# A planner's longer instruction fetch, the order of the first row loads, and the engine of the memory copy in a 68-step recurrent attention kernel

## The chip, the cores and the metric

The kernel runs on one core of a Trainium2 chip. A core has TensorE (PE in the profile; its weight loads are a row of their own, PEld), VectorE (DVE), ScalarE (ACT), GpSimd (POOL), SyncE (SP, which here only issues transfers) and 16 DMA engines. The metric is the device time of one execution in microseconds (us). Seven executions of the kernel before lie between 1632.25 and 1633.52 us, with a median of 1632.38 us.

## The reference

Four layers follow one another on a sequence of 2048 rows of 512 bf16 values: attention with a carried memory, a dense layer, the same attention again, the same dense layer again. Each reads the layer norm of its input and adds to it.

```python
for s in range(64):                                   # 64 segments of 32 rows
    h = concat([mem, xs])                             # 8 memory rows + 32 rows of the segment
    q, k, v = h @ Wq, h @ Wk, h @ Wv                  # 32 heads of 128
    p = softmax(where(mask, q @ k.T * scale, -1e9))
    o = (p @ v) @ Wo                                  # 40 x 512
    mem = o[:8]; outs.append(o[8:])                   # the memory goes into the next segment
x = x + attention(layernorm(x), mem0)
x = x + relu(layernorm(x) @ w1) @ w2                  # inner width 1376
# ... and both once more
```

The memory makes the segments of one attention layer a chain: a segment's queries, keys and values need the eight rows that the segment before it left.

## The kernel before

The two attention layers run side by side, the second four segments (DELTA) behind the first, so there are 68 steps. In steps 0 to 3 only the first is active, in steps 64 to 67 only the second, between them both. A step holds, for five units of heads (UNITS: u0 to u4): projections of queries and keys (`queries_keys`, PE line 667), values (`values`, PE line 1000), scores (line 1084), the softmax on DVE and ACT (`block`, `top`, `sub`, `exp`, `total`, `recip`, `mul`: lines 1095 to 1126), the turning of the probabilities on PE (`scores.turn`) with two masked copies out of PSUM (`keep`, lines 1149 on ACT and 1151 on DVE), the product with the values (`attend`, line 1168), and the output projection (`project`, PE into the bank `st`). In odd steps a pair of segments is finished and its dense layer begins; that work is spread over the next step too. The last matmuls of a dense layer (`dense_layer.mm.3` to `.5`) stream 512 columns each.

At a step's end `project` leaves the new memory in `st`, and one copy (`ev`, line 1212, on DVE: 128 x 64 values when both layers are active) brings its rows into HT, from which the next step's queries and keys are made. The rows of the segment itself are copied after it (`rows`, on ACT or DVE).

At the start, the weights come in through POOL's queue (Wv, then Wq, Wk and Wo in two pieces each; Wv's first quarter through SP). The rows of group 0 (128 rows) and the initial memory come through ACT's queue (`get_x`, `get_memory`, lines 619 and 622), as do the rows of groups 1 to 7 (`load`, line 827), into two buffers in turn. In steps 0 and 1 the values of those seven groups are made ahead of time (`*values`, PE line 1000), kept in the room of w1 and w2, and stored to DRAM by POOL (lines 838 and 963); then SP loads w1 and w2 into that room (`load_dense`).

Nothing of the order is written out by hand. `Plan.order` is a list scheduler: each operation has a cost on each engine that may do it, latencies between engines (LAT), and a priority from the tables PLACE, AHEAD and PERIOD. It walks through planned time, takes the operation of least priority that can start, and so fixes the order on every engine, the engine of each copy that either ACT or DVE may do (`copy_op`), and, for the operations in PAIRED, whether PE does a product in one go over 128 columns of weights or in two halves of 64 (twice the instructions; a change between the two shapes is a switch, planned at TURN). The planned times are used for nothing else. PE's instructions are modelled in `order` too: every 64 pairs of weight load and matmul are a block, and a block is not planned to end sooner than FETCH (7.0 us) after the fourth block before it.

Of the kernel before, what the change touches and what calls it, by code (L numbers as in the profile page):

```python
# [28 lines left out]
BLOCK, FETCH = 64, 7.0  # L29

RULE = (0.0714, 334.5336, 21842.5159, 2217302446.7678)
PERIOD = 40.244
PLACE = {
    ("attend.mmu0.0", 0): 609.348, ("attend.mmu0.0", 1): -183.486, ("attend.mmu0.0", 2): 147.437,
    ("attend.mmu0.0", 3): -78.515, ("attend.mmu0.0", 4): 65.61, ("attend.mmu0.0", 5): 366.858,
    ("attend.mmu0.0", 6): -249.718, ("attend.mmu1.0", 0): 726.903, ("attend.mmu1.0", 1): 684.118,
    ("attend.mmu1.0", 2): -19.8, ("attend.mmu1.0", 3): 132.658, ("attend.mmu1.0", 4): 129.759,
    ("attend.mmu1.0", 5): 371.411, ("attend.mmu1.0", 6): -353.4, ("attend.mmu2.0", 0): -14.873,
    ("attend.mmu2.0", 1): -1055.665, ("attend.mmu2.0", 2): 375.184, ("attend.mmu2.0", 3): 495.749,
    ("attend.mmu2.0", 4): 267.365, ("attend.mmu2.0", 5): 143.496, ("attend.mmu2.0", 6): -164.881,  # L40
    ("attend.mmu3.0", 0): 55.83, ("attend.mmu3.0", 1): 304.958, ("attend.mmu3.0", 2): -27.575,
    ("attend.mmu3.0", 3): 521.565, ("attend.mmu3.0", 4): -53.654, ("attend.mmu3.0", 5): -33.75,
    ("attend.mmu3.0", 6): 139.713, ("attend.mmu4.0", 0): -1004.936, ("attend.mmu4.0", 1): -1157.418,
    ("attend.mmu4.0", 2): -270.186, ("attend.mmu4.0", 3): -964.038, ("attend.mmu4.0", 4): -328.51,
    ("attend.mmu4.0", 5): 58.406, ("attend.mmu4.0", 6): -138.434, ("dense_layer.mm.0", 1): 844.726,
    ("dense_layer.mm.0", 3): 771.51, ("dense_layer.mm.0", 6): 794.222, ("dense_layer.mm.1", 1): 595.059,
    ("dense_layer.mm.1", 3): 282.976, ("dense_layer.mm.1", 6): -365.611, ("dense_layer.mm.2", 1): 402.759,
    ("dense_layer.mm.2", 3): 201.475, ("dense_layer.mm.2", 6): 383.89, ("dense_layer.mm.3", 1): 375.463,
    ("dense_layer.mm.3", 3): 375.816, ("dense_layer.mm.3", 6): 544.49, ("dense_layer.mm.4", 1): -1179.846,
    ("dense_layer.mm.4", 3): -271.405, ("dense_layer.mm.4", 6): -220.579, ("dense_layer.mm.5", 1): 907.374,  # L50
    ("dense_layer.mm.5", 3): 373.845, ("dense_layer.mm.5", 6): 565.451, ("finish_pair.turn.0", 1): -90.833,
    ("finish_pair.turn.0", 3): -375.688, ("finish_pair.turn.0", 6): -738.706, ("g0", 2): -581.803,
    ("g1", 2): -1043.701, ("g2", 2): 282.751, ("g3", 2): -205.545, ("g4", 2): 584.676, ("g5", 2): -60.649,
    ("g6", 2): 371.668, ("g7", 2): 288.938, ("late_values.mmv0.0", 0): -64.904, ("late_values.mmv1.0", 0): 678.294,
    ("late_values.mmv2.0", 0): 101.482, ("late_values.mmv3.0", 0): 44.512, ("late_values.mmv4.0", 0): 351.071,
    ("late_values.mmv5.0", 0): -24.294, ("late_values.mmv6.0", 0): -120.477, ("late_values.mmv7.0", 0): -996.402,
    ("layernorm.turn.0", 1): 92.873, ("layernorm.turn.0", 3): -23.204, ("layernorm.turn.0", 6): 193.698,
    ("layernorm.turn.1", 1): 910.291, ("layernorm.turn.1", 3): -857.558, ("layernorm.turnr.0", 0): -337.322,
    ("layernorm.turnr.1", 0): -831.277, ("prepare.turns.0", 2): 390.358, ("project.mm.0", 0): 359.615,
    ("project.mm.0", 1): -869.571, ("project.mm.0", 2): -60.568, ("project.mm.0", 3): -169.635,  # L60
    ("project.mm.0", 4): 156.569, ("project.mm.0", 5): 430.997, ("project.mm.0", 6): -293.953,
    ("project.mm.1", 0): 824.231, ("project.mm.1", 1): 252.725, ("project.mm.1", 2): 43.429,
    ("project.mm.1", 3): 540.792, ("project.mm.1", 4): -164.609, ("project.mm.1", 5): 588.5,
    ("project.mm.1", 6): 101.76, ("project.mm.2", 0): 126.782, ("project.mm.2", 1): -862.581,
    ("project.mm.2", 2): -235.851, ("project.mm.2", 3): 70.544, ("project.mm.2", 4): -259.138,
    ("project.mm.2", 5): -117.671, ("project.mm.2", 6): -300.67, ("project.mm.3", 0): 223.614,
    ("project.mm.3", 1): -213.188, ("project.mm.3", 2): -93.552, ("project.mm.3", 3): 545.141,
    ("project.mm.3", 4): 351.716, ("project.mm.3", 5): -238.608, ("project.mm.3", 6): -107.853,
    ("project.mm.4", 0): 230.883, ("project.mm.4", 1): -148.91, ("project.mm.4", 2): -568.124,
    ("project.mm.4", 3): 379.873, ("project.mm.4", 4): -132.884, ("project.mm.4", 5): 770.552,  # L70
    ("project.mm.4", 6): 66.643, ("queries_keys.mmu0.0", 0): -119.1, ("queries_keys.mmu0.0", 1): -850.808,
    ("queries_keys.mmu0.0", 2): -204.722, ("queries_keys.mmu0.0", 3): -113.926, ("queries_keys.mmu0.0", 4): 59.817,
    ("queries_keys.mmu0.0", 5): -235.287, ("queries_keys.mmu0.0", 6): -320.902,
    ("queries_keys.mmu0.1", 0): -402.058, ("queries_keys.mmu0.1", 1): 10.017, ("queries_keys.mmu0.1", 2): 261.017,
    ("queries_keys.mmu0.1", 3): -213.134, ("queries_keys.mmu0.1", 4): -297.361, ("queries_keys.mmu0.1", 5): -84.629,
    ("queries_keys.mmu0.1", 6): -888.993, ("queries_keys.mmu0.2", 0): -392.541,
    ("queries_keys.mmu0.2", 1): -333.397, ("queries_keys.mmu0.2", 2): -356.282, ("queries_keys.mmu0.2", 3): -51.387,
    ("queries_keys.mmu0.2", 4): -331.518, ("queries_keys.mmu0.2", 5): -853.492,
    ("queries_keys.mmu0.2", 6): -1044.343, ("queries_keys.mmu0.3", 0): -40.65, ("queries_keys.mmu0.3", 1): -57.543,
    ("queries_keys.mmu0.3", 2): -41.34, ("queries_keys.mmu0.3", 3): -1060.763, ("queries_keys.mmu0.3", 4): -376.858,  # L80
    ("queries_keys.mmu0.3", 5): -120.052, ("queries_keys.mmu0.3", 6): -111.195,
    ("queries_keys.mmu1.0", 0): -259.357, ("queries_keys.mmu1.0", 1): -373.272, ("queries_keys.mmu1.0", 2): 371.489,
    ("queries_keys.mmu1.0", 3): -1015.198, ("queries_keys.mmu1.0", 4): 169.449,
    ("queries_keys.mmu1.0", 5): -376.609, ("queries_keys.mmu1.0", 6): -35.359, ("queries_keys.mmu1.1", 0): -890.304,
    ("queries_keys.mmu1.1", 1): -52.862, ("queries_keys.mmu1.1", 2): 261.214, ("queries_keys.mmu1.1", 3): -931.873,
    ("queries_keys.mmu1.1", 4): -80.004, ("queries_keys.mmu1.1", 5): -905.415, ("queries_keys.mmu1.1", 6): -75.569,
    ("queries_keys.mmu1.2", 0): -1032.537, ("queries_keys.mmu1.2", 1): -941.562,
    ("queries_keys.mmu1.2", 2): -245.647, ("queries_keys.mmu1.2", 3): -738.459, ("queries_keys.mmu1.2", 4): 282.479,
    ("queries_keys.mmu1.2", 5): -47.448, ("queries_keys.mmu1.2", 6): -355.274, ("queries_keys.mmu1.3", 0): -1042.76,
    ("queries_keys.mmu1.3", 1): -311.787, ("queries_keys.mmu1.3", 2): -329.768,  # L90
    ("queries_keys.mmu1.3", 3): -856.085, ("queries_keys.mmu1.3", 4): -47.655, ("queries_keys.mmu1.3", 5): -394.586,
    ("queries_keys.mmu1.3", 6): -257.527, ("queries_keys.mmu2.0", 0): -51.901, ("queries_keys.mmu2.0", 1): -283.405,
    ("queries_keys.mmu2.0", 2): -257.559, ("queries_keys.mmu2.0", 3): 302.184, ("queries_keys.mmu2.0", 4): 98.406,
    ("queries_keys.mmu2.0", 5): 305.605, ("queries_keys.mmu2.0", 6): 363.104, ("queries_keys.mmu2.1", 0): -34.459,
    ("queries_keys.mmu2.1", 1): 44.98, ("queries_keys.mmu2.1", 2): 334.384, ("queries_keys.mmu2.1", 3): -1093.708,
    ("queries_keys.mmu2.1", 4): -293.392, ("queries_keys.mmu2.1", 5): 351.704,
    ("queries_keys.mmu2.1", 6): -1178.673, ("queries_keys.mmu2.2", 0): -41.303, ("queries_keys.mmu2.2", 1): 58.94,
    ("queries_keys.mmu2.2", 2): 291.775, ("queries_keys.mmu2.2", 3): 52.266, ("queries_keys.mmu2.2", 4): -151.786,
    ("queries_keys.mmu2.2", 5): 228.689, ("queries_keys.mmu2.2", 6): 405.936, ("queries_keys.mmu2.3", 0): 330.979,
    ("queries_keys.mmu2.3", 1): 57.914, ("queries_keys.mmu2.3", 2): -40.37, ("queries_keys.mmu2.3", 3): 87.416,  # L100
# [1234 lines left out]
```

## Time and profile before

| | us |
|---|---|
| profiled execution, whole | 1633.52 |
| its span, first to last instruction | 1631.8 |
| PE busy | 1588.3 (97%), 43116 matmuls |
| DVE busy | 1045.8 (64%) |
| ACT busy | 1077.9 (66%) |
| POOL busy | 139.6 (9%) |
| end of step 0, 1, 2, 3 | 56.27, 74.06, 95.55, 113.69 |
| a steady even step, a steady odd step | 24.82, 22.5 to 23.2 |
| median of seven executions | 1632.38 |

A step's end is the start of the first weight load after the last one of `project`. In the views below, "A <- B" means that A waited and B released it. A line is that of the helper that issued the instruction, so PE's line 667 covers projections, turnings and dense products alike, told apart by the tile that they write (work, st, fill). "Issue" is a wait for which the profile shows no releaser. PEclk is the granted clock of PE, 1.00 being full speed. Counting instructions gives one more measure: PE's weight loads are all in the trace, in the order of the program, so each planned operation can be found with its start.

### The profile page before, as it was taken

The numbers are of one execution on the slowest core, as the hardware profiler recorded it, in microseconds if no ns is written. First come the engines' busy times: TensorE is split into PE (matmuls) and PEld (weight loads), VectorE is DVE, ScalarE is ACT, GpSimd is POOL, SyncE is SP. The second block draws the span as 40 slices with busy tenths as digits, with TensorE's granted clock in tenths as the row PEclk, the third lists the DMA queues.
The fourth block names the chain that finished last, engine by engine and source line by source line (L and its number), as shares of the span: only waits on it lengthen the run. The fifth ranks groups of instructions, "written<-read, shape, count | busy, mean of one in ns | idle before, by whom it ended". The sixth has DMA issues, their size and how long they took to land.

```text
span 1631.8 us, 94544 instructions
## 1 busy us (share of the span) xinstructions
PE 1588.3 (97%) x43116; PEld 1381.0 (85%) x43179; DVE 1045.8 (64%) x3025; ACT 1077.9 (66%) x2717; POOL 139.6 (9%) x363
## 2 busy tenths in 40 slices
PE   7999999999999999999999999999999999999997
PEld 4778888888888888888888888888888888888886
DVE  4556656666765676676567567656656765665664
ACT  4556766766666676666667667666666666676654
POOL 4210000001000000100000000000000000000000
PEclk9999999999999999999999999999999999999998
DMA  9521001111100110111011111101101000000000
GB/s 372 198 82 35 19 23 28 25 25 35 31 23 21 30 25 25 35 28 26 22 30 25 25 35 28 25 23 28 26 25 26 25 19 19 20 18 19 16 6 6
DMA packets 42881, 63.30 MB, mean 39 GB/s; under 512 B 15401, under 2 KB 28817, under 8 KB 42481
## 3 DMA queue, kind: packets, MB, share of 16 engines
q1 hardware_dynamic: 35984, 35.88, 9.0%
q0 software_dynamic: 5328, 20.32, 3.3%
q8 instruction: 338, 5.54, 1.4%
q10 hardware_dynamic: 1168, 1.06, 0.2%
q14 instruction: 63, 0.51, 0.1%
HBM read 33.50 MB, written 11.93 MB: 28 GB/s over the span
## 4 chain that ended last, share of the span: by engine, by line
PE 92%; DVE 4%; DMA 1%; issue 1%; ACT 1%; POOL 0%; DVEq 0%; POOLq 0%; ACTq 0%; SPq 0%
PE work L667 38%; PE st L667 19%; PE fill L1000 15%; PE fill L667 12%; PE work L1168 4%; PE work L1084 3%; DMA hT<-in_A_x_dram 1%; DVE es L1095 1%; DVE sm L1109 1%; DVE mx L1099 1%; DVE P L1126 0%; DVE es L1102 0%; DVE HT L1212 0%; PE fill L791 0%; DMA xb<-in_A_x_dram 0%
## 5 line engine op out<-in xcount | busy, mean ns | idle before, releaser
L667 PE MATMUL work<-HT,Wk_sb 128*128 128x80 bf16 (+2 forms) x10144 | 363.7, 200 | 9.9 <-DVE HT L1212 9.2
L667 PE MATMUL work<-HT,Wq_sb 128*128 128x80 bf16 (+2 forms) x9728 | 361.7, 200 | 0.3 <-DVE HT L1212 0.2
L667 PEld LDWEIGHTS <-Wk_sb 128*128 128x128 bf16 (+1 forms) x10144 | 330.9, 103 | 29.9 <-DVE HT L1212 12.8
L667 PE MATMUL st<-OT,Wo_sb 128*128 128x80 bf16 (+1 forms) x8704 | 339.3, 199 | 1.9 <-ACT OT L921 1.3
L667 PEld LDWEIGHTS <-Wq_sb 128*128 128x128 bf16 (+1 forms) x9728 | 327.1, 102 | 13.4 <-DVE HT L1212 5.0
L667 PEld LDWEIGHTS <-Wo_sb 128*128 128x128 bf16 x8704 | 319.1, 99 | 11.0 <-issue 4.0
L1000 PE MATMUL fill<-Wv_sb,HT 128*64 128x512 bf16 x2176 | 274.0, 383 | 0.0
L921 ACT CAST kT<-work 128x320 bf16<-128x320 f32 (+1 forms) x537 | 219.4, 409 | 71.6 <-PE work L667 35.1
L921 ACT CAST qT<-work 128x320 bf16<-128x320 f32 (+1 forms) x484 | 197.3, 408 | 103.1 <-PE work L667 58.6
L1149 ACT ACTIVATE PT<-work,half 128x160 bf16<-128x160 f32 (+2 forms) x447 | 202.6, 468 | 18.2 <-DVE PT L1151 14.1
L921 ACT CAST OT<-work 128x320 bf16<-128x320 f32 (+1 forms) x387 | 149.2, 415 | 98.0 <-PE work L1168 97.9
L921 ACT CAST vw<-fill 128x512 bf16<-128x512 f32 x229 | 134.0, 585 | 104.5 <-PE fill L1000 102.3
L1095 DVE TENSOR_TENSOR es<-work,maskb 128x320 f32<-128x320 f32 (+2 forms) x340 | 130.5, 400 | 87.6 <-PE work L1084 80.7
L1000 PEld LDWEIGHTS <-HT 128*64 128x64 bf16 x2176 | 107.3, 110 | 72.5 <-issue 1.9
L1106 ACT ACTIVATE es<-es 128x320 f32<-128x320 f32 (+2 forms) x340 | 133.2, 406 | 8.3 <-DVE es L1102 3.5
L1126 DVE TENSOR_TENSOR P<-es,sm 128x320 bf16<-128x320 f32 (+2 forms) x337 | 131.1, 405 | 4.4
L1151 DVE TENSOR_SCALAR PT<-work,half 128x320 bf16<-128x320 f32 (+2 forms) x233 | 105.0, 454 | 44.5 <-PE work L667 42.6
L1102 DVE TENSOR_TENSOR es<-es,mx 128x320 f32<-128x320 f32 (+2 forms) x340 | 131.5, 403 | 1.5
L1099 DVE TENSOR_REDUCE mx<-es 128x8 f32<-128x320 f32 (+2 forms) x340 | 129.5, 397 | 2.8
L1109 DVE TENSOR_REDUCE sm<-es 128x8 f32<-128x320 f32 (+2 forms) x340 | 128.4, 393 | 1.8 <-ACT es L1106 1.7
L1212 DVE CAST HT<-st 128x64 bf16<-128x64 f32 (+1 forms) x67 | 14.8, 220 | 162.9 <-PE st L667 162.6
L1168 PE MATMUL work<-PT,vw 128*64 128x80 bf16 (+1 forms) x1384 | 106.0, 202 | 1.7 <-DVE PT L1151 1.7
(99 smaller groups left out, 1730.9 us busy)
## 6 DMA issues: line engine op xcount, KB each, us to landing
V<-vw SPq DMA_DIRECT2D x240, 48.0 KB
V<-vh SPq DMA_DIRECT2D x120, 64.0 KB
Wq_sb<-in_A_Wq_dram POOLq DMA_DIRECT2D x2, 2048.0 KB, 20.2
Wk_sb<-in_A_Wk_dram POOLq DMA_DIRECT2D x2, 2048.0 KB, 24.6
Wo_sb<-in_A_Wo_dram POOLq DMA_DIRECT2D x2, 2048.0 KB, 35.8
vh<-vg SPq DMA_DIRECT2D x32, 128.0 KB
Wv_sb<-in_A_Wv_dram POOLq DMA_DIRECT2D x1, 2048.0 KB, 11.5
vh<-w_sb POOLq DMA_DIRECT2D x4, 512.0 KB, 6.5
```

Source lines behind the costliest of these rows:

```text
L667: nc.tensor.matmul(out_[u:v, :], lhsT=lhsT[:, u:v], rhs=rhs, start=start, stop=stop, tile_position=(0, u), **more)
L921: nc.scalar.copy(out=out_, in_=in_)
L1000: nc.tensor.matmul(vp[64 * b:64 * b + 64, :], lhsT=cols(c4), rhs=Wv_sb[:, c4, n * 512:(n + 1) * 512], start=(c4 == 0), stop=(c4 == NC4 - 1 ...
L1095: nc.vector.tensor_tensor(out=flat(es[:, A]), in0=flat(sp[:, A]), op=ALU.add, in1=maskb[:, a_lo:a_hi, :].unsqueeze(2).to_broadcast([128, n ...
L1099: nc.vector.tensor_reduce(out=mx[:, As], in_=es3(), axis=AX.X, op=ALU.max)
L1102: nc.vector.tensor_tensor(out=es3(), in0=es3(), op=ALU.subtract, in1=mx[:, As].unsqueeze(2).to_broadcast([128, ns * na, L]))
L1106: nc.scalar.activation(out=es[:, A], in_=es[:, A], func=ACTF.Exp, scale=SCALE)
L1109: nc.vector.tensor_reduce(out=sm[:, As], in_=es3(), axis=AX.X, op=ALU.add)
L1126: (nc.gpsimd if eng == POOL else nc.vector).tensor_tensor(out=o, in0=flat(es[:, A]), op=ALU.mult, in1=sm[:, As].rearrange("p (a s) -> p a ...
L1149: nc.scalar.activation(out=o, in_=i, func=ACTF.Copy, scale=half[:, b:b + 1])
L1151: nc.vector.tensor_scalar_mul(out=o, in0=i, scalar1=half[:, b:b + 1])
L1168: nc.tensor.matmul(o[u:u + cols, :, a, :], lhsT=V[:, p, e0 + u:e0 + u + cols], rhs=PT[:, a, 2 * i + h2, :, :], start=True, stop=True, tile ...
```

## The change

- The plan's constant FETCH stays 7.0 us after 100 us of planned time, and is 9.5 us before (LOADED).
- `get_memory` is planned after `get_x`, and the loads of the rows of groups 1 to 7 are planned after `get_memory`. These are edges in the plan only; on the chip they are the order of three issues in ACT's queue.
- The copy of the new memory into HT becomes a `copy_op`: the plan may give it to ACT or DVE.
- RULE, PERIOD, PLACE, PAIRED and AHEAD hold new numbers.

```diff
-BLOCK, FETCH = 64, 7.0
+BLOCK, FETCH, LOADED = 64, 7.0, (100.0, 9.5)
-RULE = (0.0714, 334.5336, 21842.5159, 2217302446.7678)
-PERIOD = 40.244
+RULE = (0.0673, 328.8783, 6739.3694, 3962424687.5956)
+PERIOD = 38.4534
 PLACE = {
...
 PAIRED = {
...
 AHEAD = {
...
                 for i in range(issued // BLOCK + 1, (issued + n) // BLOCK + 1):
-                    t1 += max(0.0, blocks[-4] + FETCH - (t1 + o.cost[e] * (i * BLOCK - issued) / n))
+                    t1 += max(0.0, blocks[-4] + (FETCH if t > LOADED[0] else LOADED[1]) - (t1 + o.cost[e] * (i * BLOCK - issued) / n))
...
-        plan.op(ACT, 0.45, get_x, w=[xb0])
-        plan.op(ACT, 0.45, get_memory, w=[mb0])
+        plan.op(ACT, 0.45, get_x, w=[xb0, "x0"])
+        plan.op(ACT, 0.45, get_memory, r=["x0"], w=[mb0, "start"])
...
-            plan.op(*((ACT, 0.45) if early else (SP, 0.78)), load, r=[*gate, *(rows if g > 1 else [])],
+            plan.op(*((ACT, 0.45) if early else (SP, 0.78)), load, r=[*gate, *(["start"] if early else []), *(rows if g > 1 else [])],
...
-            def ev():
-                nc.vector.tensor_copy(out=HTn[:, :, m_lo:m_hi], in_=v(2 * W)[:, :, m_lo:m_hi])
+            def ev(eng):
+                copy_on(eng, HTn[:, :, m_lo:m_hi], v(2 * W)[:, :, m_lo:m_hi])
 
-            plan.op(DVE, 0.15, ev, r=[wo], w=[("HTm", i), ("taken", k)])
+            copy_op(64, ev, r=[wo], w=[("HTm", i), ("taken", k)], more={ACT: 0.01, DVE: 0.02})
```

`copy_on` and `copy_op` are as before: the first calls `nc.scalar.copy` or `nc.vector.tensor_copy`, the second plans an operation that ACT or DVE may do.

As built, the two programs do the same 3101 operations on PE. All 67 memory copies are ACT's in the changed program. PE has 44197 pairs of weight load and matmul instead of 43179, because 60 query and key projections and 17 other products are done in halves that were whole, and 24 products are whole that were in halves; switches between the two shapes are 297 instead of 305.

## The prediction

> **What bounds the kernel now.** I read the page first (engine shares, chain), then the releasers of PE's waits, then stretches of the start, of a steady step's end and of the last step.
>
> ```profile
> PE 1588.3 (97%) x43116; PEld 1381.0 (85%) x43179; DVE 1045.8 (64%) x3025; ACT 1077.9 (66%) x2717; POOL 139.6 (9%) x363
> q8 instruction: 338, 5.54, 1.4%
> PE 92%; DVE 4%; DMA 1%; issue 1%; ACT 1%; POOL 0%; DVEq 0%; POOLq 0%; ACTq 0%; SPq 0%
> ```
>
> PE is the bound: 97% busy and 92% of the chain. So an edit is worth what it takes from PE's work or from its pauses. Queue q8 carries 5.54 MB in 338 packets, 16,384 bytes each, which is PE's program of 86,500 instructions: one packet holds 256 instructions, 128 pairs of weight load and matmul.
>
> PE's pauses lie in three places. First, the loading steps. The timeline of PE, and windows (width, then PE and PEld busy, further engines, granted clock, DMA share, GB/s):
>
> ```profile
> 82.27 0.22 PE L1084 MATMUL work<-kT,qT 128*40 128x40 bf16 x3
> 84.78 0.23 PE L1084 MATMUL work<-kT,qT 128*40 128x40 bf16 x5 [2.29 <-issue]
> ```
> ```profile
> 37.44:44.14 6.70, 5.91 (x136) 4.18 (x132) 4.16 (x13) 4.09 (x11) 0.79 (x2) 1.00 1.02 349
> 78.31:84.78 6.47, 4.18 (x128) 3.53 (x128) 3.70 (x14) 2.75 (x10) 0.18 (x1) 1.00 1.02 310
> 85.56:88.98 3.42, 3.42 (x57) 2.30 (x55) 2.53 (x10) 2.32 (x8) 0.00 (x0) 0.50 1.04 364
> ```
>
> PE stops in the middle of an operation, with no releaser. Such stops (43.4, 78.0, 82.3, 129.8 us and a few later) all fall on the same place of a block of 256 instructions, and PE goes on 1.3 to 1.6 us after a q8 packet has ended. That packet starts only when PE has crossed the block's beginning. So 128 pairs can't take less than the wait for the packet's start, plus about 1.1 us, plus 1.45. I call that sum the need. Measured crossing by crossing it was 5.3, 6.0, 6.7, 6.3, 4.7 us from 23.6 to 56 us and 4.2, 6.3, 6.4 at 74.1, 78.3, 84.8, when the DMA share is 1.0; 3.5 at 91; from 116 us on the median is 2.98 and 95% lie under 3.66. The last window shows PE at half clock just after the long stop.
>
> Second, the end of an odd step (timeline, start and length first):
>
> ```profile
> 925.98 0.22 DVE L1212 CAST HT<-st 128x64 bf16<-128x64 f32 x1 [1.96 <-PE st L667]
> 926.24 0.37 ACT L921 CAST OX<-st 128x256 bf16<-128x256 f32 x1 [1.08 <-DVE HT L1212]
> 926.26 0.62 PEld L667 LDWEIGHTS <-Wk_sb 128*128 128x128 bf16 x16 [0.45 <-DVE HT L1212]
> ```
>
> From the last weight load of `project` to the copy's start are 274 ns, the copy takes 224, PE's next weight load comes 52 later: 550. At even ends the last dense matmuls cover that. At 30 odd ends PE stands still.
>
> Third, the last steps, bound by the softmax on DVE (DVE's timeline in step 67):
>
> ```profile
> 1611.02 0.49 DVE L1095 TENSOR_TENSOR es<-work,maskb 128x80 f32<-128x80 f32 x2
> 1613.18 0.46 DVE L1126 TENSOR_TENSOR P<-es,sm 128x80 bf16<-128x80 f32 x2
> 1614.25 0.75 DVE L1151 TENSOR_SCALAR PT<-work,half 128x80 bf16<-128x80 f32 x2
> ```
>
> Units u2 and u3 go through DVE back to back, and PE waits for their masked copies (1.06 and 0.48 us in `attend`).
>
> **The change part by part**, against the profiled execution's 1633.5 us (span 1631.8, 1.7 around it). That execution is the slowest of seven; the median is 1.1 lower, so I put the difference on 1632.4.
>
> *Steady steps, the order.* Steps 5 to 63 keep each step's set of products and four switches a step; a few neighbours change place. In even steps DVE takes the masked copies of u3 and u4 (0.38 us each, 0.30 apart) before `attend` of u3. From u3's turning: 0.27 to start, two more behind it, 0.05 to PE: ready after 1.30 us. Meanwhile PE does u2's `attend` (0.29), one `project` unit (1.15) and u4's `attend` (0.14), and comes at 1.61. So this costs nothing while `project` stands between; without it 1.1 us, 29 times. In odd steps u2's and u3's query copies swap engines. Zero for the order.
>
> *The memory copy.* ACT's cast of 128x64 is not in the trace; its nearest rows, by form:
>
> ```profile
> L1212 DVE CAST HT<-st 128x64 bf16<-128x64 f32 x60 | 13.4, 224 | 150.6 <-PE st L667 150.3
> L921 ACT CAST OX<-st 128x256 bf16<-128x256 f32 x57 | 21.2, 372 | 95.1 <-DVE HT L1212 95.1
> L921 ACT CAST OX<-st 128x128 bf16<-128x128 f32 x2 | 0.5, 265 | 2.7 <-DVE HT L1212 2.1 <-PE st L667 0.6
> ```
>
> 372 at 256 and 265 at 128 give 0.84 ns a value, so 212 at 64. PE to ACT is 273 ns (query copies), ACT to PE 51 to 55 (turnings behind late values): as for DVE. So 30 x -12 ns = -0.4 us; bounds 190 and 265 ns, -1.0 to +1.2. ACT is idle there (1.08 us before OX), and what is queued behind the copy, OX and the next queries, waited for it anyway.
>
> *The first loads.* Group 0's rows go out at 0.79 instead of 1.25 us, the memory at 1.25 instead of 1.73, group 1's after both. Group 0's chain begins some 0.3 us sooner, but POOL now issues both pieces (0.82 us each) before group 1's `power`, so the first values start at about 12.2 against 12.34. What shrinks are waits up to 31 us: 1.7 between values, 0.6 among the first projections. -1.4; bounds -2.0 and +0.5.
>
> *Instruction fetch while the weights load.* The block begun at about 37 us holds, before, 74 projections of 25 ns and 24 values of 108 (4.4 with what else is in it 5.4) and took 6.7. After it holds 115 projections, 8 products of 36 and 4 turnings: 3.5 us. With the same need of 6.7 PE stands 3.2 instead of 1.3: +1.9; bounds 0 (its packet finds the queue as free as at 50 us) and +2.4. A stop of 3 us may halve the clock as at 85.56: 3.4 us at half cost 1.7. [...]
>
> *The stores.* POOL's store of group 4's values, and six stores behind it, wait for the last of those values; PE makes it before step 1's end now, after it in the changed order. POOL's burst begins near 75.7 instead of 72.2, SP's loads of w1 and w2 (78.21 to 83.7, landed by 91) some 3.5 later, and the other transfers queued on SP with them, which step 4 needs 15 us later. Before, blocks 9 to 12 took 20.8 us for 16.0 of work (4.8 lost). After they hold 3.4, 4.5, 4.8, 3.5 us; the middle two meet the need of 6.3 and 6.4 (1.8 + 1.6), the last meets the burst's end (0 to 2.9, I take 1.5). +0.1; bounds -1.5 and +2.0. The first dense product comes near 92 us, where w1 has just landed.
>
> *Steps 3 to 5.* Step 3's waits (0.6) may go; a block of step 4 with `project` in halves holds 2.6 us, under the need: +0.5. Zero, bounds 0.7 either way.
>
> *Instruction fetch in steady steps.* 32 more pairs in an odd step make dense blocks denser. Blocks shorter than 3.3 us after step 4: 17 before, 25 after. Every block's shortfall against the measured needs, averaged, sums to 2.9 us before and 4.9 after; the stops that the trace has come to 1.7, so I scale the difference by 0.6: +1.2; bounds 0 and +2.5.
>
> *The last steps.* Steps 65 and 67 have four switches fewer each (107 ns a pair of in and out by `queries_keys`, 0.43 a step, hidden where DVE binds), but u2's scores come about 1.2 us sooner since one values block now follows them, and a `project` unit (0.8) stands between turnings and `attend`. DVE gets a copy of 0.69 in place of one of 0.32. 0.9 a step: -1.8; bounds -2.6 and -0.5.
>
> Sum: -0.4 - 1.4 + 1.9 + 0.8 + 0.1 + 0 + 1.2 - 1.8 = **+0.4 us: 1632.8**.
>
> [...]
>
> **The rivals.**
> - *The plan's 9.5 us is two blocks' measure, and PE pays per block* (slower): the block at 37 us costs its 2.4, the clock 1.7, the shifted burst 2.0, steady blocks 2.5, less 3.6 of gains: +5, 1637.4. It decides if the packet fetched at 37 us starts over 4 us after its crossing, as 4.1 before. For it: the needs above. Against: blocks 3 and 4 after it are long (6.5, 6.4) and take the packets with room. Chance 0.18.
> - *The longer fetch spreads the work as meant* (faster): none of the 1.3 + 4.8 us of stops is left, the rest as summed (-0.4 - 1.4 + 1.2 - 1.8): -8 at most, with half the stops -5: 1627.4. Against: blocks of 3.4 to 4.8 us against a need of 6.3. Chance 0.13.
> - *ACT's copy is no cheaper* (265 ns or more, as its 128-wide one): +1.2 and more, inside the range. Chance 0.03 that it alone passes 3.3 us: 110 ns more at 30 ends.
> - *The loading edges do nothing*: the landings differ by 0.3 us anyway. It is contained in -1.4.
>
> **How the numbers follow.** 0.2% is 3.3 us, about what a measurement of this kernel can tell from no change. The sum as worked out, within 3.3 us either way: 0.66; its own range 1630 to 1636. Slower: 0.18 + 0.03 = 0.21. Faster: 0.13. The range reaches to both rivals: 1628.5 to 1638.5.
>
> **What would show it.** Right: the memory copy on ACT near 212 ns and 540 ns from last `project` load to PE; a PE stop of 2.5 to 3.5 us by "issue" at 40 to 45 us; half clock behind it or not; POOL's stores from about 75.7; steady steps at 24.8 and 22.5 to 23.3; step 67 about 0.9 shorter. Wrong: no stop near 42 us or steps 0 to 3 ending before 112 us (then the second rival), even steps over 25 us (the u3 copies), or ACT busy when `st` is done.

## The result and the profile after

The changed kernel takes 1636.53 us (median of 15 runs, 1634.38 to 1637.44) against 1632.25 of the kernel before (35 runs): 4.3 us or 0.26% slower, ratio 1.0026, 95% interval 1.0020 to 1.0033. The time lies in the predicted range (1628.5 to 1638.5), 3.7 us above the predicted 1632.8, and nearer to the slower rival (1637.4) than to the forecast. The profiled execution took 1636.88 us with a span of 1635.2, against 1633.52 and 1631.8 before, where it was the slowest of the 35: 3.4 us between the two traces. The mean granted clock is 0.994 or 0.995 in every execution of the changed kernel, 0.995 in the profiled one.

The page of the changed kernel, engine shares, the instruction queue and the chain:

```profile
PE 1589.2 (97%) x44129; PEld 1381.2 (84%) x44197; DVE 1059.0 (65%) x3008; ACT 1066.3 (65%) x2734; POOL 139.7 (9%) x363
q8 instruction: 346, 5.67, 1.4%
PE 91%; DMA 3%; DVE 2%; ACT 1%; issue 1%; POOL 0%; SPq 0%; POOLq 0%; DVEq 0%; ACTq 0%
```

PE's work is the same within 1 us. What has grown in the chain is the share of DMA, 1% before and 3% now. The chain in order of time says where: two of its pieces are transfers of weights, and neither is in the chain before, whose longest transfers are rows of x (7.41 and 7.71 us). The first ends at 39.43 us without a wait of PE in this trace; the second ends a long one:

```profile
7.90 31.53 DMA Wk_sb<-in_A_Wk_dram
...
85.83 10.10 DMA w_sb<-in_B_w_dram
```

The timeline of PE in step 2 (start, length, then in brackets the idle time before and what ended it), first of the kernel before, then of the changed one:

```profile
90.49 0.97 PE L667 MATMUL st<-OT,Wo_sb 128*128 128x40 bf16 x32
91.31 0.63 PE L667 MATMUL fill<-xnM,w_sb 128*128 128x64 bf16 x16
```
```profile
91.38 0.20 PE L668 MATMUL work<-ident,P 128*128 128x80 bf16 x1
95.98 1.25 PE L668 MATMUL fill<-xnM,w_sb 128*128 128x64 bf16 x20 [4.40 <-DMA w_sb<-in_B_w_dram]
```

PE comes to the first dense product at the same time in both, 91.3 and 91.6 us. Before, w1 had landed at 88.70 us, 2.6 us ahead of the product (the last update of the semaphore of its fourth piece). After, it lands at 95.93, 4.4 us after PE has come, and PE stands. Windows of the changed kernel around it (width, PE, PEld, DVE, ACT, POOL busy, granted clock, DMA share, GB/s):

```profile
90.84:94.26 3.42, 0.74 (x27) 0.60 (x23) 0.73 (x3) 0.77 (x3) 0.00 (x0) 1.00 1.06 378
94.26:97.67 3.41, 1.69 (x31) 1.70 (x32) 0.00 (x0) 0.38 (x1) 0.00 (x0) 0.50 0.48 133
97.67:101.09 3.42, 3.21 (x84) 3.09 (x81) 0.22 (x1) 1.02 (x5) 0.00 (x0) 0.50 0.03 7
```

From 94.26 us, within the wait, the granted clock is 0.5 for 6.83 us, 5.1 of them behind the wait. So the 20 dense products of the row after take 1.25 us, 62 ns each, where the 16 of the row before took 0.63, 39 ns each.

Where the 3.4 us between the two spans come from, by step ends (the last weight load of `project` to the next load; the step's length after less that before). Since a few products change their step, the third column is an estimate that takes out the nominal time of what moved, worked out for each product from its usual duration in the trace:

| stretch | length, after - before | with the moved work taken out | running sum |
|---|---|---|---|
| step 0 | -0.04 | +1.0 | +1.0 |
| step 1 | +1.35 | +1.0 | +2.1 |
| step 2 | +4.30 | +3.4 | +5.5 |
| steps 3 and 4 | +1.14 | +1.25 | +6.75 |
| steps 5 to 63 | -0.54 | -0.54 | +6.2 |
| steps 64 to 67 | -2.0 | -2.0 | +4.2 |
| tail | -0.8 | -0.8 | +3.4 |

So the steady steps and the end gain, and the loading steps lose twice as much. Of step 1's loss 0.75 us are waits of PE for the probabilities (P, from DVE), of which it had none there before.

### The profile page after: what moved, and what is told of

It reads as the page before. It is cut to its first block, busy times and chain, and to the rows that moved or that the text cites. A ratio compares the mean times of both kernels' runs of the same rounds, so it can differ in the third digit from the quotient of the medians.

```text
span 1635.2 us, 96828 instructions
## 1 busy us (share of the span) xinstructions
PE 1589.2 (97%) x44129; PEld 1381.2 (84%) x44197; DVE 1059.0 (65%) x3008; ACT 1066.3 (65%) x2734; POOL 139.7 (9%) x363
## 4 chain that ended last, share of the span: by engine, by line
PE 91%; DMA 3%; DVE 2%; ACT 1%; issue 1%; POOL 0%; SPq 0%; POOLq 0%; DVEq 0%; ACTq 0%
PE work L668 39%; PE st L668 18%; PE fill L1001 14%; PE fill L668 12%; PE work L1169 4%; PE work L1085 3%; DMA Wk_sb<-in_A_Wk_dram 2%; DMA w_sb<-in_B_w_dram 1%; DMA V<-vw 0%; ACT HT L922 0%; PE fill L792 0%; DVE es L1096 0%; DVE mx L1100 0%; DVE sm L1110 0%; DVE PT L1152 0%
## 5 line engine op out<-in xcount | busy, mean ns | idle before, releaser
L668 PE MATMUL work<-HT,Wq_sb 128*128 128x80 bf16 (+2 forms) x10208 | 366.6, 200 | 8.4 <-ACT HT L922 8.4
L668 PE MATMUL work<-HT,Wk_sb 128*128 128x80 bf16 (+2 forms) x10624 | 368.5, 200 | 2.6 <-issue 1.6
L668 PE MATMUL st<-OT,Wo_sb 128*128 128x80 bf16 (+2 forms) x8768 | 341.5, 199 | 2.1 <-ACT OT L922 0.9
L668 PEld LDWEIGHTS <-Wo_sb 128*128 128x128 bf16 (+1 forms) x8768 | 320.6, 100 | 10.8 <-issue 3.2
L1150 ACT ACTIVATE PT<-work,half 128x320 bf16<-128x320 f32 (+1 forms) x365 | 174.0, 486 | 68.7 <-PE work L668 54.6
L1152 DVE TENSOR_SCALAR PT<-work,half 128x160 bf16<-128x160 f32 (+2 forms) x315 | 130.6, 433 | 53.9 <-PE work L668 52.1
L887 DVE TENSOR_TENSOR xg<-xg,fill 128x512 f32<-128x512 f32 (+1 forms) x34 | 23.3, 687 | 187.3 <-PE fill L668 181.1
L1085 PEld LDWEIGHTS <-qT 128*40 128x40 bf16 x4096 | 84.5, 98 | 29.0 <-issue 0.5
```

Of the source, the lines that this page charges most:

```text
L668: nc.tensor.matmul(out_[u:v, :], lhsT=lhsT[:, u:v], rhs=rhs, start=start, stop=stop, tile_position=(0, u), **more)
L1085: nc.tensor.matmul(v[64 * g2:64 * g2 + L, a, i, b, :], lhsT=qT[:, hi, a * L:(a + 1) * L], rhs=kT[:, hi, a * L:(a + 1) * L], start=True, st ...
L1150: nc.scalar.activation(out=o, in_=i, func=ACTF.Copy, scale=half[:, b:b + 1])
L1152: nc.vector.tensor_scalar_mul(out=o, in0=i, scalar1=half[:, b:b + 1])
```

## The experiments

But for the mixed kernel and the two with another plan setting, each was made without a new plan: either one line of the emitted code was changed, or single operations were moved in the finished order, just before it is emitted, by this helper (numbers are the operations' sequence numbers):

```python
ops = plan.order()

def move(seqs, before=None, after=None):
    at = {o.seq: o for o in ops}
    for q in seqs:
        ops.remove(at[q])
    i = ops.index(at[after]) + 1 if before is None else ops.index(at[before])
    ops[i:i] = [at[q] for q in seqs]
```

Medians are given beside that of the kernel before measured with it (1631.3 to 1631.6 us in these runs, 1632.25 beside the changed kernel).

### The memory copy alone

```diff
             def ev():
-                nc.vector.tensor_copy(out=HTn[:, :, m_lo:m_hi], in_=v(2 * W)[:, :, m_lo:m_hi])
+                nc.scalar.copy(out=HTn[:, :, m_lo:m_hi], in_=v(2 * W)[:, :, m_lo:m_hi])
```

> The kernel before, with nothing changed but the engine of the memory copy (ACT instead of DVE, all steps). Theory of the prediction: at the 30 odd step ends PE gets its next weight load sooner by the difference of the two copies, 212 against 224 ns; the changed kernel's trace has its odd steps 0.03 to 0.04 us shorter, so 30 to 31 times that: 0.9 to 1.2 us less than before (ratio 0.9993 to 0.9995). Rival: the shorter odd steps of the changed kernel come from its other order, and the copy alone gives 12 ns x 30 = 0.4 us or nothing; odd steps then stay at 22.67 and 23.23.

Measured: 1631.31 us beside 1631.58, ratio 1.0000 (0.9991 to 1.0009). The copies of this kernel and an odd step's end:

```profile
L1212 ACT CAST HT<-st x67: 186/213/213, 56.1 to 1598.2; 128x64 bf16<-128x64 f32 x60, 128x32 bf16<-128x32 f32 x7
```
```profile
923.56 0.21 ACT L1212 CAST HT<-st 128x64 bf16<-128x64 f32 x1 [0.82 <-PE st L667]
923.83 0.61 PEld L667 LDWEIGHTS <-Wk_sb 128*128 128x128 bf16 x16 [0.44 <-ACT HT L1212]
```

The copy takes 213 ns in place of 224; the estimate was 212. From `project`'s last weight load to PE's next it is 536 ns in place of 551 (median of 27 odd ends in each trace; 536 in the changed kernel too): 15 ns, 0.4 to 0.45 us in all. That is the rival's number, and mine of the prediction; the expectation had read too much into odd steps that are 0.03 to 0.04 us shorter in the changed kernel, half of which belongs to its other order. A gain of 0.4 us is too small for this timing to confirm.

### The order of the first loads alone

On ACT's queue group 1's rows come behind group 0's rows and the memory, in the kernel before: `move([44], after=19)`.

> The kernel before, with only ACT's three first transfers in the changed kernel's order (group 0's rows, the memory, then group 1's rows). Theory of the prediction: group 0's chain begins up to 1.2 us sooner (the changed kernel's first power at 6.19 instead of 7.52 us, first values at 11.16 instead of 12.33), and the step ends shift by 1.0 to 1.4 us from step 0 on, ratio 0.9992. Rival: the weights' landing and the instruction packets of 23 to 50 us set step 0's end whatever the first chain does; step 0 then ends at 56.0 to 56.3 as before and the median does not move.

Measured: 1629.96 us beside 1631.28, ratio 0.9989 (0.9980 to 0.9999). POOL's first `power` and PE's first values, in the kernel before, then in this one:

```profile
7.52 0.23 POOL L714 TENSOR_SCALAR ln<-ln 128x1 f32<-128x1 f32 x1 [1.34 <-DVE ln L711]
12.34 3.62 PE L1000 MATMUL fill<-Wv_sb,xg 128*64 128x512 bf16 x16 [0.68 <-ACT xg L921]
```
```profile
6.19 0.26 POOL L714 TENSOR_SCALAR ln<-ln 128x1 f32<-128x1 f32 x1
10.69 3.62 PE L1000 MATMUL fill<-Wv_sb,xg 128*64 128x512 bf16 x16 [0.68 <-ACT xg L921]
```

Group 0's `power` starts at 6.19 us instead of 7.52, PE's first values at 10.69 instead of 12.34, and step 0 ends 1.9 us sooner in this trace; the rival falls. The gain is this start: PE's waits between the first values and 31 us are what they were (0.39 and 0.45 us before `xg` in both traces).

### The changed order from step 5 on, behind the old start

Both sets of tables, the old one for steps 0 to 4, and the old loads and plan settings; PE's order is that of the kernel before through step 3 and that of the changed kernel from step 5 on:

```diff
-                o.prio = PERIOD * o.step + PLACE.get((o.key, phase(o.step)), 0.0)
+                o.prio = (PERIOD * o.step + PLACE.get((o.key, phase(o.step)), 0.0) if o.step > LAST else
+                          OLD_PERIOD * o.step + OLD_PLACE.get((o.key, phase(o.step)), 0.0))
...
-            copy_op(64, ev, r=[wo], w=[("HTm", i), ("taken", k)], more={ACT: 0.01, DVE: 0.02})
+            if k > LAST:
+                copy_op(64, ev, r=[wo], w=[("HTm", i), ("taken", k)], more={ACT: 0.01, DVE: 0.02})
+            else:
+                plan.op(DVE, 0.15, ev0, r=[wo], w=[("HTm", i), ("taken", k)])
```

> The changed kernel's order from step 5 on, behind the order of the kernel before for steps 0 to 3 (step 4 is planned anew between them, loads as before, memory copy of steps 0 to 4 on DVE). Theory: all of the loss lies in steps 0 to 4 (+6.75 us by the end of step 4 in the two traces), and what follows is a gain of 0.5 (steps 5 to 63) and 2.8 us (last steps and tail): 3.3 us under before, about 1629 us, ratio 0.998. Rival: the order of the steady steps costs PE's instruction fetch what the last steps give (my +1.2), and the trace of the changed kernel had a lucky run of packets: 1631 to 1632.

Measured: 1628.58 us beside 1631.58, ratio 0.9983 (0.9974 to 0.9991): 3.0 us faster than before, 3.3 were expected. All of the loss of the changed kernel lies in its loading steps, and the rest of the change is worth some 3 us. Steps 65 and 67 take 16.91 and 16.73 us as in the changed kernel (18.06 and 17.80 before).

### The plan's longer fetch alone

The kernel before with one setting of the plan changed (`BLOCK, FETCH, LOADED = 64, 7.0, (100.0, 9.5)` and its use); steps 1 to 4 are reordered.

> The kernel before, tables and loads unchanged, with only the plan's longer instruction fetch (9.5 instead of 7.0 in the first 100 us of the plan). It reorders steps 1 to 4, step 0 keeps its order, steps from 5 on keep theirs. If the longer fetch by itself spreads the work as meant, the stop of 2.3 us at 82.3 and its half clock go and steps 1 to 4 end 2 to 5 us sooner. If the plan only believes in longer blocks, it shuffles: the blocks between 70 and 95 us hold 4.1, 3.3, 4.4, 4.3 us of work in place of 3.3, 3.3, 4.0, 5.2 against a need of 4.2 to 6.4, so about the same stops, within 2 us of before at step 4's end, with the place of the stops changed; a wait for w1 is possible where the stores move behind step 1.

Measured: 1637.04 us beside 1631.28, ratio 1.0035 (1.0021 to 1.0048), 5.8 us slower. The waits of PE in steps 1 to 4 of this kernel (what was waited for: total us, times, longest):

```profile
PE fill L667 <- DMA w_sb<-in_B_w_dram: 2.9, 1, 2.9
```

The stop of 2.3 us at 82.3 is gone, as was meant, and in its place PE stands 2.9 us for w1 at 88.9 us with 3.41 us of half clock behind it, as there was behind the stop. In this order the first dense product stands 14 pairs sooner than before; POOL's burst begins at 74.2 instead of 72.2 us, a `layernorm` operation stands ahead of its last store, and SP's loads begin at 80.3 instead of 78.2, and two pieces of w2 instead of one stand ahead of w1's fourth. The possible wait for w1 in the expectation was the outcome, not a side remark. It does not account for all: against the stop that it replaces, the wait costs 0.6 us, and steps 1 to 4 are 4.6 us longer in this trace, with the same 2272 pairs. PE's idle time in them grows by 2.7 us (4.2 to 6.9), mostly in short waits; the rest is open. With four executions the interval of the setting alone reaches from 3.4 to 7.8 us, so it costs about as much as the whole change or more.

### The changed kernel with the old fetch

```diff
-BLOCK, FETCH, LOADED = 64, 7.0, (100.0, 9.5)
+BLOCK, FETCH, LOADED = 64, 7.0, (100.0, 7.0)
```

> The changed kernel with the plan's fetch in the loading steps back at 7.0 us (tables, loads and memory copy as changed). Step 0 keeps its order, steps 1 to 4 are planned anew; the first dense product is planned behind one project unit instead of two, group 4's last value before two of step 1's project units. Theory (the wait for w1 is made by the loads' lag behind the order, not by the number alone): PE comes to the first dense product near 88 us and w1 lands some 19 us after POOL's burst starts, so near 92 to 93: a stop of 3 to 4.5 us with half clock again, within 2 us of the changed kernel's 1636.5. Rival (the longer fetch in the plan is the whole cause): no wait for w1, 1630 to 1632.

Measured: 1631.95 us beside 1631.59, ratio 1.0004 (0.9995 to 1.0013). PE's wait in this kernel:

```profile
PE fill L668 <- DMA w_sb<-in_B_w_dram: 1.7, 1, 1.7
```

Neither expectation holds whole. The wait for w1 is there, so the number is not its only cause; but it is 1.7 us instead of 4.4 and no half clock follows in this execution. It is the fastest of the ten, with a mean granted clock of 0.998; in others it goes down to 0.995, so half clock does come in them. POOL's stores go out in one burst from 72.2 to 76.5 us here, as before, and w1 has landed at 90.1. Some 2 us of this trace's distance to the changed kernel's lie in step 0, which has the same order in both but no half clock here, 2.1 in step 2 and 2.4 in steps 3 and 4; what makes the last is open.

### What holds w1 back: the order on SP's queue, the stores on POOL's

The issues of SP and of POOL in the kernel before:

```profile
78.21 1.48 SPq L529 DMA_DIRECT2D w_sb<-in_B_w_dram  x2
79.79 0.54 SPq L534 DMA_DIRECT2D w_sb<-in_B_w_dram  x1
80.37 1.36 SPq L529 DMA_DIRECT2D w_sb<-in_B_w_dram  x2
```
```profile
74.92 0.54 POOL L963 DMA_DIRECT2D vh<-vg  x1
75.46 0.54 POOL L838 DMA_DIRECT2D xh<-OX  x1
75.99 0.54 POOL L963 DMA_DIRECT2D vh<-vw  x1
77.62 0.22 POOL L714 TENSOR_SCALAR ln<-ln 64x1 f32<-64x1 f32 x1 [1.09 <-DVE ln L711]
```

and in the changed kernel (L530 loads a piece of w1, L535 of w2):

```profile
82.08 1.17 SPq L530 DMA_DIRECT2D w_sb<-in_B_w_dram  x2
83.35 1.82 SPq L535 DMA_DIRECT2D w_sb<-in_B_w_dram  x2
85.22 2.21 SPq L530 DMA_DIRECT2D w_sb<-in_B_w_dram  x2
```
```profile
77.34 0.54 POOL L964 DMA_DIRECT2D vh<-w_sb  x1 [7.36 <-ACT kT L922]
...
79.47 0.54 POOL L839 DMA_DIRECT2D xh<-xg  x1
81.17 0.22 POOL L715 TENSOR_SCALAR ln<-ln 64x1 f32<-64x1 f32 x1 [1.16 <-DVE ln L712]
81.48 0.57 POOL L716 TENSOR_TENSOR ln<-ln,mhalf 64x1 f32<-64x1 f32 x1
82.01 0.62 POOL L964 DMA_DIRECT2D vh<-vg  x1
82.64 0.56 POOL L839 DMA_DIRECT2D xh<-OX  x1
83.19 0.54 POOL L964 DMA_DIRECT2D vh<-vw  x1
```

w1's first piece is issued 3.9 us later than before, its fourth 4.7 us later (85.83 instead of 81.10), and it takes 10.1 us to land instead of 7.6, so that w1 lands 7.2 us later. Three things have come together. The burst begins 5.1 us later (77.34). A second piece of w2 stands ahead of w1's last two. And a `layernorm` operation, which waits for DVE until 81.17, now stands in the middle of POOL's queue, so the stores of groups 6 and 7 go out at 82 to 84 us beside w1. POOL's DMA queue moved its last stores by 81.5 us before; in the changed kernel it moves 1.2 MB more between 84 and 90 us, while SP's moves 0.26 to 0.42 MB per 2 us in place of 0.6 to 0.76. Three runs take these apart.

SP's order (the two pieces of w2 behind w1's fourth): `move([401, 477], after=325)` in the changed kernel.

> The changed kernel; only on SP's queue the two pieces of w2 that stood between w1's second and third piece come behind w1's fourth. Theory A (order): PE's stop of 4.4 us before the first dense product at 91.6 us is the wait for w1's last two pieces, which were issued at 85.2 to 87.4 behind 0.5 MB each of w2; now issued by about 85, landed by about 91: stop under 1 us, no half clock at 94 to 101 us, 5 to 6.5 us less than the changed kernel, 1630 to 1631.5. Theory B (late stores): SP can't begin before 82.1 since the stores of group 5's values hold w1's room, and the transfers behind them fill the queues anyway: stop stays over 2.5 us, half clock stays, at most 2 us gained, 1634.5 to 1636.5.

Measured: 1631.47 us beside 1631.58, ratio 0.9999 (0.9990 to 1.0008). PE in this kernel:

```profile
90.40 1.05 PE L668 MATMUL fill<-xnM,w_sb 128*128 128x64 bf16 x28 [1.22 <-DMA w_sb<-in_B_w_dram]
...
94.52 0.42 PE L668 MATMUL st<-OT,Wo_sb 128*128 128x40 bf16 x10 [1.17 <-issue]
```

The median is in theory A's range, theory B's (1634.5 to 1636.5) is missed. But the trace is not all A's: 1.2 us of the wait stay, a stop for the program (1.17, "issue") appears 3 us later, and the granted clock is 0.50 from 96.03 to 99.44 us. Step 2 is 3.6 us shorter than in the changed kernel; another 2.3 of this trace's distance lie in step 0, where this execution had no half clock (on that see the stop at 41 us below).

The stores of group 5, on which w1's room hangs, ahead of group 4's as well: `move([311, 313, 315], before=309)` and the move above.

> As the run before, and on POOL's queue the stores of group 5's rows and values come ahead of that of group 4's values, for which POOL stood until 77.3 us. Both theories: w1's room is free near 75 us, w1 is issued from there, landed by about 86, no stop at 91 us. It tells how much more than the order of SP's queue the late burst costs: theory A, the same as the run before within 1 us; theory B, 5 us or more better than the changed kernel only here. In either case w2's pieces are issued from about 81 us, and a new wait of the second dense products for w2 (near 107 us) would show in the waits of PE.

Measured: 1630.84 us beside 1631.58, ratio 0.9993 (0.9984 to 1.0002). w1 is issued from 74.89 us, PE never waits for it, step 2 is 4.5 us shorter than in the changed kernel. In its place stands a stop of 1.55 us at 85 us:

```profile
86.52 0.28 PE L668 MATMUL work<-ident,P 128*128 128x80 bf16 x3 [1.55 <-issue]
```

So SP's order is worth most of what there was to gain here, the earlier room about 1 us more in step 2; the medians of the two differ by less than their intervals.

The stores of groups 6 and 7 (1 MB) behind everything: `move([319, 323], after=570)` in the changed kernel, SP's order as changed.

> The changed kernel with POOL's stores of the values of groups 6 and 7 moved behind the loads of w1 and w2 (to about 110 us); SP's order as changed, so w1's last two pieces still stand behind two pieces of w2. If the volume in the queues (1 MB of stores) decides when w1 lands: w1 lands near 93, the stop of 4.4 us becomes 1 to 2 us and the kernel takes 1632 to 1634. If SP's order alone decides: the stop stays over 3.5 us, 1635 to 1636.5.

Measured: 1632.59 us beside 1631.59, ratio 1.0006 (0.9997 to 1.0015). The waits of PE between 80 and 105 us:

```profile
PE st L668 <- issue: 1.2, 1, 1.2
PE fill L668 <- DMA w_sb<-in_B_w_dram: 0.8, 1, 0.8
```

w1 lands at 92.1 with SP's order untouched, 3.9 us sooner than in the changed kernel. But this execution had no half clock in step 0 and ended it 2.1 us sooner; counted from the end of step 0, w1 lands 1.8 us sooner here and 3.2 us sooner in the run with only SP's order changed (39.7 us in the changed kernel, 37.9 and 36.5). The wait is as short as it is because PE itself comes 1.8 us later by the same count, after the stop of 1.2 us and at half clock, which lasts 6.83 us from 89.13. Step 2 is 2.0 us shorter than in the changed kernel, against 3.6 with SP's order. So both matter, and in these traces the place in the queue matters more; the medians of the two runs differ by less than their intervals. What the two moves give together no run shows.

### The program's fetch: the stop at 41 us, and the stores

The stop that the prediction placed in the block begun at 37 us is there, in the changed kernel:

```profile
42.77 0.52 PE L668 MATMUL work<-HT,Wk_sb 128*128 128x40 bf16 x13 [1.63 <-issue]
```

One product of group 4's values and its copy were moved ahead into that block, in the changed kernel: `move([96, 97], before=200)`.

> The changed kernel, with one values product of group 4 (8 pairs of 86 to 108 ns) and its copy moved from behind PE's stop at 41.2 us to 38.2 us, into the block of 128 pairs that the stop ends. Fetch theory: that block's own work grows by about 0.66 us and a pair of switches (0.2), so the stop of 1.6 us shrinks to 0.6 to 0.9 at the same time of its end; the period before 43 us holds less idle time and the half clock after it (3.41 us, 1.7 lost) goes: step 0 ends at 54.5 to 55 instead of 56.2, and 1.4 to 1.7 us are gained. Rival (the stop waits for something else, data or a queue): the stop keeps its length or only moves, nothing gained. A caution: one run of the same order in this block (with only SP's queue changed) had the stop in two parts and no half clock, so the half clock alone is no proof.

Measured: 1634.17 us beside 1631.28, ratio 1.0016 (1.0007 to 1.0025), where the changed kernel stands at 1.0026. The stop in this kernel:

```profile
42.01 0.19 PE L668 MATMUL work<-HT,Wk_sb 128*128 128x40 bf16 x1 [0.50 <-issue]
```

With 0.9 us more work in the block the stop falls from 1.63 to 0.50 us, at the same place in the program, and step 0 ends at 54.42 instead of 56.23, without half clock. In the five traces with the unedited order of step 0 this stop varies, from 0.8 to 1.9 us, and in two of them PE also waits 0.4 and 0.6 us in this block for a piece of Wk; 0.50 lies under all of them. So the stop is one for the program, and the rival falls, except that the landing of Wk can take a part. By the ratios the edit is worth 1.6 us, but the two intervals overlap. How much of the 1.8 us the edit makes is open: the half clock after this stop came in this trace not at all, in the five unedited ones twice (the changed kernel and the one with group 5 first), and not in the other three.

Then the same question where the stores and w1, w2 load. The mixed kernel with the stores of groups 6 and 7 moved to 100 us: `move([319, 323], after=570)`.

> The mixed kernel (start as before, rest as changed), with POOL's stores of the values of groups 6 and 7 (0.5 MB each) moved from 75 us to about 100 us, where no load is under way. Theory: the packets of PE's program wait in queues that the stores and w1, w2 fill together; with 1 MB less between 75 and 91 us the needs of 4.2, 6.3 and 6.4 us at 74 to 85 us fall, w lands some 3 us sooner, the stop of 2.3 us at 82 shrinks below 1.2 and the half clock after it goes: 2 to 4 us under the mixed kernel, 1625 to 1627. Rival: w's loads fill the queues alone from 78 us on, the need of 6.3 stays and only the block after it gains: within 1 us of the mixed kernel.

Measured: 1627.40 us beside 1631.28, ratio 0.9978 (0.9967 to 0.9988). Windows of the mixed kernel, then of this one:

```profile
75.00:80.00 5.00, 5.00 (x161) 4.37 (x157) 3.13 (x9) 2.60 (x10) 1.97 (x5) 1.00 1.01 352
80.00:85.00 5.00, 2.71 (x86) 2.26 (x84) 2.56 (x12) 1.97 (x8) 0.00 (x0) 0.96 1.01 292
85.00:90.00 5.00, 5.00 (x93) 3.27 (x90) 3.53 (x16) 3.54 (x13) 0.05 (x1) 0.69 0.83 286
```
```profile
75.00:80.00 5.00, 5.00 (x164) 4.38 (x161) 2.89 (x8) 2.61 (x9) 1.23 (x3) 1.00 0.68 209
80.00:85.00 5.00, 5.00 (x150) 4.09 (x148) 4.79 (x21) 4.03 (x15) 0.00 (x0) 1.00 0.99 359
85.00:90.00 5.00, 4.15 (x124) 3.55 (x120) 3.81 (x15) 3.42 (x14) 1.51 (x3) 1.00 0.70 229
```

With the DMA share between 75 and 80 us down from 1.01 to 0.68, the packet for the block begun at 78 us is there 2.4 us sooner: its need falls from 6.56 to 4.13 us, the stop of 2.3 us at 82 and the half clock go, and step 2 is 2.7 us shorter. A stop of 0.85 at 87 us comes back. In medians it is 0.8 to 1.2 us less than the mixed kernel (by the ratios and by the times, which were measured apart), not the 2 to 4 expected, and less than the intervals can tell from nothing; what is shown is the trace.

### A version that beats both kernels

The mixed kernel with the late stores and the new order of the first loads: `move([44], after=19)`, `move([319, 323], after=570)`.

> The mixed kernel with the late stores of groups 6 and 7 and with ACT's first three transfers in the changed order. If the three gains add up: 1.2 to 1.3 us under the mixed kernel with late stores, 1626 us, ratio to before 0.997. Rival: step 0's stop at 43 us takes the earlier start back (its packet waits for the weights' transfers): 1627.4 as without.

Measured: 1625.78 us beside 1631.59, ratio 0.9967 (0.9954 to 0.9979): 5.8 us faster than before, about 10 us faster than the changed kernel by the ratios. The three gains add up as expected, within the intervals. No half clock is left ahead of the last steps.

And with group 5's stores and all of w1 ahead, on top of it (`move([311, 313, 315], before=309)`, `move([401], after=325)`):

> As the run before, and on POOL's queue the stores of group 5 ahead of that of group 4, on SP's queue all of w1 ahead of w2: w1's loads begin near 73 us instead of 78. If w's volume under the queue sets the need, it only moves to earlier blocks: blocks of 3.3 and 4.0 us at 70 to 78 us get a need of 5 to 6, the block of 6.2 at 82 gets shorter; within 1 us of the run before. If PE still waits for w1 or for its packets at 87 us, up to 1.5 us better, 1624.5 to 1626.

Measured: 1629.56 us beside 1631.59, ratio 0.9987 (0.9978 to 0.9996), 3.8 us worse than the run before in the median. In the trace step 2 is 4.7 us longer, and step 0 1.8 us shorter in the same order. PE in this kernel:

```profile
79.74 0.22 PE L1246 MATMUL work<-kT,qT 128*40 128x40 bf16 x3
82.80 0.26 PE L1246 MATMUL work<-kT,qT 128*40 128x40 bf16 x5 [2.84 <-issue]
```

w1 and w2 are issued from 71.5 to 77.1 us, and the block begun at 75.8 has a need of 7.1 us: PE stops 2.84 us and runs 6.83 us at half clock. The order that helped in the changed kernel's start is a loss in the other: the volume moved onto a block with 4.1 us of work.

## Why the prediction was right, and where it was wrong

The time fell in the range; the sum of +0.4 us was too low by 3 us against the trace of before (+3.4) and by 3.7 in the median. That the time fell in the range is in part luck: the range reached to both rivals, and terms that were too low by 3.3 (stores and w1), 1.2 (steps 3 to 5), 1.0 (step 1, which the sum left out) and 0.9 us (half clock) met others that were too high by 1.3 (steady steps, without the copy), 0.8 (the tail, left out too) and 0.8 (the block at 37 us). Point by point:

- **Memory copy, -0.4.** Right: 212 to 213 ns, 15 ns from load to load at each of 27 to 30 ends, 0.4 us.
- **First loads, -1.4.** Right in size, wrong in place: the prediction had the first values 0.1 us sooner and the rest from shorter waits up to 31 us. The first values came 1.2 us sooner in the changed kernel and 1.6 in the run with this edit alone (1.3 in its median), and the waits behind them stayed.
- **The block at 37 us, +1.9.** Right in place and kind, too large: PE's stop by "issue" is 1.63 us instead of 0.54, +1.1, and not the 2.5 to 3.5 that was to show it. The need of this block was 5.6 us in the changed kernel, not the 6.7 carried over from before; it starts earlier and its packet waited 3.1 instead of 4.1 us.
- **Half clock after it, +0.8.** The 1.7 is what 3.4 us at half clock lose; no run shows the share of it that the sum uses, which was the author's estimate. In the runs the half clock came in two of five traces with this order, and in the profiled execution, behind a stop of 1.63 us, it cost its 1.7.
- **Stores and w1, +0.1 (-1.5 to +2.0). This is the step that failed.** The prediction said that the burst would begin near 75.7, that SP's loads would follow 3.5 us later, and that "the first dense product comes near 92 us, where w1 has just landed". It came at 91.6, w1 at 95.9. With the landing of before, 88.70 us, a delay of 3.5 would put it at 92.2, beside the product; the delay was 7.2, because w1's fourth piece was issued 4.7 us later and took 2.5 us longer to land. The mis-sized part of the term is thus the landing of w1, for which the prediction had no more than the shift of the burst. The diff's order also showed the two things that made it worse, the piece of w2 ahead of w1's last two and the `layernorm` operation between the stores, and neither was priced. Step 2 grew by 4.3 us (3.4 with moved work taken out): 4.4 of wait and about 2.5 of half clock, less the 2.3 of stop and 1.7 of half clock that step 2 had before, and smaller waits.
- **Steps 3 to 5, 0 (bounds 0.7).** +1.2: outside. Two blocks of step 4, 2.95 and 3.36 us long, hold stops of 0.58 and 0.54 us by "issue"; the prediction had named one.
- **Steady fetch, +1.2 (0 to 2.5).** Too large: -0.5 in the changed kernel's trace, of which -0.4 is the copy, and -1.0 in the mixed kernel's with nearly the same order. From step 5 on PE's waits by "issue" of over 0.15 us come to 0.2 us before and to none in the changed kernel: the shortfalls that the prediction added up hardly became stops in either.
- **Last steps, -1.8.** Right: -2.0 to the end of step 67, for the cause named. PE comes to the same `attend` without a wait; before, then after:

```profile
1615.05 0.38 PE L1168 MATMUL work<-PT,vw 128*128 128x80 bf16 x6 [0.87 <-DVE PT L1151]
```
```profile
1619.28 0.38 PE L1169 MATMUL work<-PT,vw 128*128 128x80 bf16 x6
```

Another 0.8 us in the tail were not predicted: there the half clock, which before reached from 1621.56 us to the end, 10.2 us, covers 3.41 us around the dense products and the last 1.5 us now.

Of the rivals, the slower one had the right size and only part of its mechanism: the clock and the shifted burst, yes; the block at 37 us at half its price, and its packet started 3.1 us after the crossing, not over 4 as the rival asked; a per-block price in the steady steps, no; and its price for the burst left out the wait for w1. The faster rival asked what the longer fetch of the plan does: by itself it costs 5.8 us. It did take away the stop at 82 us that it was to take away. What that run shows in its place is that the loads came later (from 80.3 us instead of 78.2) and the first dense product no later (14 pairs sooner in the order), and the transfers are what PE met next: it stood 2.9 us for w1.

Stops by "issue" while transfers filled the start were 0.5, 1.2, 1.6, 2.3 and 2.8 us in these traces, and the one of 2.3 us in the mixed kernel went when 1 MB of stores was moved. The half clock starts at 43.06, 94.26 and 1626.84 us in the changed kernel, 51.20 and 1532.58 us apart, and at 85.56 and 1621.56 us before, 1536.00 apart: 15, 449 and 450 times 3.4133 us, an estimate from these five starts.

## What to carry to other kernels

When an edit delays a load, work out its landing anew, and not only by the shift of its issue: here w1's fourth piece was issued 4.7 us later, and with other transfers ahead of it and beside it took 2.5 us longer to land. Then read from the trace how much room its first consumer had. Here it was 2.6 us against a delay of 7.2; of the 4.6 us beyond the room PE stood 4.4, and 5.1 us of half clock came behind the wait. Look at what stands between transfers on the engine that issues them (here one operation waiting for DVE until 81.17 us, with three stores behind it) and at which transfers then share the time (1.2 MB of stores beside w1 between 84 and 90 us); moving 1 MB of stores that nobody needs soon took away a stop of 2.3 us and the half clock behind it. And a single number of a plan, made truer on one side only, can make the plan worse, here by 5.8 us: test it alone before tables are tuned to it.

## What was not expected of the hardware

- The need of a block of 128 pairs went with the transfers beside it: it was 6.56 us in the mixed kernel, with the DMA share at 1.01 between 75 and 80 us, and 4.13 in that with the late stores, at 0.68; it was 7.1 us in the run with all of w1 ahead, where the 2.75 MB of w1 and w2 were issued within 6 us.
- The length of a stop alone does not decide whether half clock follows. Counted in stretches of 3.4133 us back from its start, PE stood 1.63 us of the stretch before 43.06 in the changed kernel, 1.45 of that before 96.03 in the run with w1 first and 0.86 of that before 89.13 in the run with late stores, and half clock followed. The same stop of 1.74 us at the same place of the program, whole within one such stretch, was followed by it in the run with the first loads alone and not in the run with the memory copy alone; 1.55 us with group 5 first were not. What else decides stays open. The first 13 to 18 us tell nothing about this: the profile's record of the clock begins only there (at 15.75 us in the changed kernel, at 17.30 before), with 1.00, and the first values ahead of it take twice as long (424 ns apart against 213 from 15.8 us on in the changed kernel), though the windows of the profile print 1.00 for them.
